# The issue order of a linear attention and Fourier feed-forward kernel, taken from one table of operations, with fewer spare matmuls

## The chip, the cores and the metric

The kernel runs on one core of a Trainium2 chip. The metric is the device time of one launch in microseconds, the median of several runs. Six queues of instructions run side by side on the core and meet through semaphores: TensorE (PE; its weight loads are listed apart as PEld), VectorE (DVE), ScalarE (ACT), GpSimd (POOL), SyncE (SP, which here only issues DMAs) and the 16 DMA engines behind them. Each queue runs its instructions in the order in which the program issued them.

## What is computed

```python
def _attn_ref(q, k, v, g_norm):                  # q, k, v: [8, 8, 576, 64]
    kv = np.einsum('bhsd,bhse->bhde', k, v)
    out = np.einsum('bhsd,bhde->bhse', q, kv)
    rms = np.sqrt(np.mean(out * out, axis=-1, keepdims=True) + 1e-06)
    return out / rms * g_norm

def _moe_ref(x, w_ch1, w_ch2):                   # x: [8, 576, 512]
    mixed = np.real(np.fft.fft(np.fft.fft(x, axis=1), axis=2))
    u = x + mixed
    un = (u - mean(u)) / np.sqrt(var(u) + 1e-06)             # over the channels
    return u + np.maximum(un @ w_ch1, 0.0) @ w_ch2            # 512 x 2048, 2048 x 512
```

The attention output of the eight heads, side by side, is the x of the second part. The two weight matrices arrive as 64-bit floats and are decoded on the chip.

## The kernel before

**Stages.** For each batch, `plan_kv` loads k and v in pieces of 256 KB (L1164) and of 64 KB for the last 64 rows (L1174), multiplies them on PE (ps_k, L1197), copies the result to kvt on ACT and, for batch 0 only, also scales it by g_norm into kvg on DVE (L1216, which needs gb, the loaded g_norm, L1070). `plan_q_load` loads half a batch of q (qt, L1236 and L1247); `plan_q` turns it on PE with an identity matrix (ps_q, L1273) and ACT copies it out (fq). Then come the output products of q with kvt and kvg, per tile of 96 or 97 rows: `plan_first_out` for batch 0 (ps_o, L1374, one group of 16 products into each of two banks with kvt and as many with kvg; three tiles, six groups), `plan_out` for the others (L1304). ACT squares one result, DVE sums the squares (L1391, `red`), takes the inverse root in steps (L1403 to L1411) and multiplies (L1419). `plan_fold` makes even and odd sums of the rows (L1508 on DVE or POOL), each split in a high part (ACT, L1514) and a low part (L1517 on DVE or POOL). `plan_seq` and `plan_chn` multiply them on PE with the tables of the two Fourier transforms (ps_f, L1544 and further lines; the tables are loaded as draw, L1107), and `plan_turn` turns the normalised rows for the feed-forward part, again as a high (unTh, ACT L1693) and a low part (unTl, DVE L1696).

**Weights.** `plan_w` loads one piece of a weight matrix (raw, 512 KB, L936; w1/0, w1/1 and so on for columns of the first matrix, w2/0 and so on for rows of the second) and decodes it: ACT clears a bank, DVE does five steps (L946, L947, L950, L953, L956) and an addition (L1743). For w1 PE then makes the column means (ps_w, L970) and DVE takes them off (L979, the center step). ACT makes the high part (L1763), DVE or POOL the low part (L1768).

**Feed-forward.** ps_h is the product of un and a piece of w1 (L1012), acc that with w2 (L1029), each in three passes over high and low parts. The first of these stands near 79 us in the profile; the attention and the transforms of the later batches run in among them until about 620 us. In the last third, behind that, the feed-forward for the other column pieces runs from stored copies.

**Spare matmuls.** `plan_spare` adds operations that multiply a constant tile (still) by itself twice into a bank that nobody reads (ps_s, 128x512, L1084). The program before has 54 of these matmuls, in 27 pairs.

**What sets the order.** The class `Plan` takes all work of the first two thirds as operations: each has an engine, a cost in ns, a rank, the operations that it needs (`after`) and the buffers that it uses; `MOVES` adds to the ranks of named operations. `run` calls `go`, a list scheduler with a model of the engines, of one pipe of transfers and of buffers that come free; it picks for each engine that is free the operation of lowest rank that can start, and fills in a spare pair where its count of TensorE columns is low. `settle` then moves or drops single operations by the table `SHIFTS`, and `emit` issues the operations in the resulting order. `RINGS` gives the number of buffers of each kind. Each queue waits in hardware for the data and the buffers of the instruction at its head.

Of the kernel before, what the change touches and what calls it, by code (L numbers as in the profile page):

```python
# [76 lines left out]
SHIFTS = [  # L77
    ("plan_spare.go/PE/-/-", 20, 0),
    ("plan_w.<lambda>/DVE/w1/2", 3, -1),
    ("plan_w.<lambda>/DVE/w1/1", 1, -2),  # L80
    ("plan_q.take/ACT/3/11", 0, 2),
    ("plan_spare.go/PE/-/-", 18, 0),
    ("plan_spare.go/PE/-/-", 26, 0),
    ("plan_w.<lambda>/DVE/w2/2", 1, -4),
    ("plan_first_out.mean/DVE/0/1", 0, -2),
    ("plan_chn.<lambda>/DVE/1/1", 1, -6),
    ("plan_spare.go/PE/-/-", 31, 0),
    ("plan_first_out.square/ACT/0/2", 1, 9),
    ("plan_chn.<lambda>/ACT/1/2", 0, 5),
    ("plan_fold.even.go/DVE/1/1", 1, -2),  # L90
    ("plan_fold.fold/DVE/1/0", 0, -6),
    ("plan_spare.go/PE/-/-", 16, 0),
    ("plan_kv.<lambda>/POOL/2/-", 1, 9),
    ("plan_kv.<lambda>/POOL/5/-", 1, -2),
    ("plan_seq.<lambda>/PE/0/1", 0, -1),
    ("plan_turn.high/ACT/0/0", 0, -2),
    ("plan_out.red/DVE/2/1", 1, 10),
    ("plan_seq.<lambda>/PE/0/0", 1, 2),
    ("plan_q_load.load/SP/1/02", 0, 10),
    ("plan_spare.go/PE/-/-", 9, -4),  # L100
    ("plan_fold.mul/DVE/2/0", 0, -4),
    ("plan_q_load.<lambda>/SP/3/-", 0, 1),
    ("plan_spare.go/PE/-/-", 27, 0),
    ("plan_out.<lambda>/ACT/2/1", 0, -1),
    ("plan_kv.<lambda>/DVE/0/-", 0, 9),
    ("plan_fold.zero/ACT/1/1", 0, 4),
    ("plan_out.<lambda>/ACT/2/1", 1, 1),
    ("plan_first.<lambda>/PE/e0/-", 9, 3),
    ("plan_chn.put.<lambda>/SP/0/0", 1, 2),
    ("plan_kv.<lambda>/SP/1/-", 8, 1),  # L110
    ("plan_fold.zero/ACT/2/2", 0, -1),
    ("plan_chn.mix/DVE/0/0", 1, 5),
    ("plan_y.last/DVE/2/-", 0, -1),
    ("plan_seq.<lambda>/PE/0/0", 0, -2),
    ("plan_out.<lambda>/ACT/1/0", 1, 4),
    ("plan_kv.go/PE/1/-", 1, 1),
    ("plan_w.<lambda>/ACT/w2/0", 0, 9),
    ("plan_first.<lambda>/PE/e0/-", 4, 1),
    ("plan_first_out.mean/DVE/0/2", 0, 1),
    ("plan_first_out.mul/DVE/0/1", 0, 1),  # L120
    ("plan_early.<lambda>/ACT/e0/-", 3, -4),
    ("plan_out.scale/POOL/1/2", 0, 8),
    ("plan_chn.<lambda>/DVE/0/0", 0, 1),
    ("plan_kv.<lambda>/SP/5/-", 8, -2),
    ("plan_q.turn/PE/2/12", 0, 1),
    ("plan_fold.fold/DVE/0/2", 0, -2),
    ("plan_kv.<lambda>/POOL/2/-", 0, 9),
    ("plan_spare.go/PE/-/-", 28, 0),
    ("plan_chn.mix/DVE/1/1", 0, -1),
    ("plan_kv.<lambda>/SP/5/-", 3, 4),  # L130
    ("plan_seq.mm/PE/1/3", 0, -2),
    ("plan_turn.high/ACT/0/0", 1, -2),
    ("plan_out.<lambda>/ACT/2/1", 0, 1),
    ("plan_fold.even.go/POOL/2/0", 1, 3),
    ("plan_fold.low/POOL/1/2", 0, -2),
    ("plan_q.take/ACT/2/11", 0, 7),
# [24 lines left out]
    ("plan_spare.go/PE/-/-", 19, 0),
    ("plan_turn.low/DVE/0/1", 2, -1),
    ("plan_first.<lambda>/PE/e0/-", 0, -2),
    ("plan_turn.high/ACT/4/0", 2, 4),
    ("plan_out.red/DVE/2/1", 1, -3),
    ("plan_kv.<lambda>/POOL/3/-", 0, 1),
    ("plan_kv.<lambda>/ACT/6/-", 0, -2),
    ("plan_q.turn/PE/7/02", 0, 1),
    ("plan_chn.add_r/POOL/5/1", 0, -1),
    ("plan_early.<lambda>/ACT/e1/-", 7, 1),  # L170
    ("plan_y.recip/DVE/4/-", 0, -2),
    ("plan_early.<lambda>/ACT/e2/-", 5, -3),
    ("plan_fold.<lambda>/ACT/2/0", 0, -4),
    ("plan_turn.low/DVE/1/2", 0, 3),
    ("plan_out.red/DVE/6/2", 0, 1),
    ("plan_q.take/ACT/7/10", 0, 1),
    ("plan_first.<lambda>/PE/e2/-", 3, -1),
    ("plan_kv.<lambda>/SP/3/-", 9, -3),
    ("plan_out.mm/PE/3/2", 0, 6),
    ("plan_out.scale/POOL/4/2", 0, -3),  # L180
    ("plan_fold.<lambda>/ACT/3/1", 0, 9),
    ("plan_out.mm/PE/4/0", 0, 1),
    ("plan_chn.<lambda>/DVE/2/2", 1, 2),
    ("plan_chn.<lambda>/DVE/4/0", 0, 4),
    ("plan_first.<lambda>/PE/e3/-", 11, -6),
    ("plan_early.<lambda>/PE/e1/-", 7, -1),
    ("plan_early.<lambda>/ACT/e3/-", 3, -3),
    ("plan_out.og/ACT/6/1", 0, -7),
    ("plan_q.take/ACT/4/11", 0, -10),
    ("plan_turn.turn/PE/1/1", 0, 2),  # L190
    ("plan_seq.mm/PE/3/3", 0, 3),
    ("plan_chn.add_l/POOL/5/1", 0, 1),
    ("plan_seq.low/DVE/3/1", 0, -1),
    ("plan_q_load.load/SP/3/-", 0, 4),
    ("plan_kv.<lambda>/SP/4/-", 4, 2),
    ("plan_early.<lambda>/ACT/e1/-", 3, 1),
    ("plan_chn.<lambda>/DVE/0/0", 1, 9),
    ("plan_seq.mm/PE/3/0", 0, 2),
    ("plan_seq.mm/PE/3/2", 0, 3),
    ("plan_fold.<lambda>/ACT/3/1", 0, 4),  # L200
    ("plan_first.<lambda>/ACT/e3/-", 1, -1),
    ("plan_fold.low/DVE/1/1", 0, -1),
    ("plan_seq.<lambda>/ACT/2/1", 0, -2),
    ("plan_q.take/ACT/2/11", 0, -3),
    ("plan_turn.high/ACT/2/0", 3, 2),
    ("plan_turn.high/ACT/3/0", 3, 1),
    ("plan_chn.add_r/POOL/5/1", 0, -1),
    ("plan_out.<lambda>/ACT/6/0", 0, -2),
    ("plan_fold.<lambda>/ACT/1/1", 0, -4),
    ("plan_fold.low/DVE/2/2", 0, -2),  # L210
    ("plan_turn.low/DVE/1/1", 2, -1),
    ("plan_chn.<lambda>/DVE/3/2", 0, -3),
    ("plan_first.<lambda>/ACT/e2/-", 2, -2),
    ("plan_y.last/DVE/2/-", 0, -3),
    ("plan_kv.<lambda>/POOL/4/-", 1, 3),
# [372 lines left out]
class Plan:  # L588

    HOP = 160  # L590
# [5 lines left out]
    SLIP = 100  # L596
# [1928 lines left out]
```

## Time and profile before

| what | value |
|---|---|
| median of 3 runs | 995.82 us (995.66 to 995.9) |
| span of the profiled execution, first to last instruction | 993.5 us |
| TensorE busy | 982.3 us (99%) |
| VectorE busy | 690.1 us (69%) |
| ScalarE, GpSimd busy | 363.4, 397.6 us |
| moved by DMA | 166.06 MB, 167 GB/s on average |

The profile is of one execution. Times are microseconds from the first instruction. In a timeline a row is a run of like instructions: its start, its length, the engine, line, operation, tile names with the shape, the count, and in brackets the idle time ahead of it and what ended that. PEclk is the TensorE clock that the chip granted, 1.00 for 2.4 GHz and 0.50 for 1.2 GHz, as a mean over the stretch.

### The profile page before, as it was taken

The numbers are of one execution on the slowest core, as the hardware profiler recorded it, in microseconds if no ns is written. First come the engines' busy times: TensorE is split into PE (matmuls) and PEld (weight loads), VectorE is DVE, ScalarE is ACT, GpSimd is POOL, SyncE is SP. The second block draws the span as 40 slices with busy tenths as digits, with TensorE's granted clock in tenths as the row PEclk, the third lists the DMA queues.
The fourth block names the chain that finished last, engine by engine and source line by source line (L and its number), as shares of the span: only waits on it lengthen the run. The fifth ranks groups of instructions, "written<-read, shape, count | busy, mean of one in ns | idle before, by whom it ended". The sixth has DMA issues, their size and how long they took to land.

```text
span 993.5 us, 17707 instructions
## 1 busy us (share of the span) xinstructions
PE 982.3 (99%) x6838; PEld 858.5 (86%) x6838; DVE 690.1 (69%) x1365; ACT 363.4 (37%) x731; POOL 397.6 (40%) x391
## 2 busy tenths in 40 slices
PE   8999999999999999999999999999999999999998
PEld 6888989988988888888888898989898888989897
DVE  4889886966667668767843786767676766767543
ACT  2466555655544333333332331323231313122221
POOL 1345443553554101434230372727272727263540
PEclk9899999999999999999999999999999999999999
DMA  9989797764453645565644515151525253424031
GB/s 231 236 222 271 210 275 230 200 161 165 144 195 117 267 168 192 181 252 211 225 170 159 201 44 212 44 212 53 202 81 187 100 171 115 153 107 149 1 127 43
DMA packets 111240, 166.06 MB, mean 167 GB/s; under 512 B 43710, under 2 KB 71666, under 8 KB 104756
## 3 DMA queue, kind: packets, MB, share of 16 engines
q1 hardware_dynamic: 103908, 149.06, 46.9%
q10 hardware_dynamic: 5328, 9.57, 2.6%
q0 software_dynamic: 1920, 6.29, 1.6%
q8 instruction: 54, 0.88, 0.4%
q14 instruction: 30, 0.25, 0.1%
HBM read 108.25 MB, written 56.64 MB: 166 GB/s over the span
## 4 chain that ended last, share of the span: by engine, by line
PE 94%; DMA 3%; SPq 1%; DVE 1%; issue 0%; ACT 0%; DVEq 0%; ACTq 0%
PE acc L1029 40%; PE ps_h L1012 20%; PE ps_h L2251 18%; PE ps_f L1586 4%; PE ps_f L1532 3%; PE ps_o L1304 3%; PE ps_k L1197 2%; PE ps_t L1684 2%; DMA vm<-in_v_dram 1%; PE ps_q L1279 1%; DMA draw<-in_dft_s_dram 1%; DMA qt<-in_q_dram 1%; PE ps_s L1084 1%; PE ps_o L1374 0%; SPq L1174 0%
## 5 line engine op out<-in xcount | busy, mean ns | idle before, releaser
L1029 PE MATMUL acc<-w,hh 128*128 128x512 f32 x1150 | 359.3, 394 | 0.0
L1029 PEld LDWEIGHTS acc<-w,hh 128*128 128x128 f32 x1150 | 205.7, 189 | 34.2
L1029 PE MATMUL acc<-w,hl 128*128 128x512 f32 x575 | 224.0, 390 | 0.0
L1021 ACT ACTIVATE hh<-ps_h 128x512 fp32r<-128x512 f32 x144 | 86.2, 598 | 345.8 <-DVE ps_h L2259 170.9
L1012 PE MATMUL ps_h<-unTh,w 128*128 128x512 f32 x576 | 179.3, 392 | 0.0
L1024 DVE SCALAR_TENSOR_TENSOR hl<-ps_h,hh 128x512 fp32r<-128x512 f32 x144 | 98.0, 684 | 92.1 <-ACT hh L1021 91.8
L1029 PEld LDWEIGHTS acc<-w,hl 128*128 128x128 f32 x575 | 108.0, 188 | 23.6
L1012 PEld LDWEIGHTS ps_h<-unTh,w 128*128 128x128 f32 x576 | 106.6, 188 | 21.3
L1012 PE MATMUL ps_h<-unTl,w 128*128 128x512 f32 x288 | 112.3, 390 | 0.0
L2211 POOL TENSOR_TENSOR up<-up 128x512 f32<-128x512 f32 x36 | 46.6, 1295 | 154.4 <-DMA up<-next_scr 119.2
L2259 DVE TENSOR_TENSOR ps_h<-part,ps_h 128x256 f32<-128x256 f32 x144 | 61.1, 425 | 40.9 <-ACT part L2264 23.3
L2259 DVE TENSOR_TENSOR part<-part,ps_h 128x256 f32<-128x256 f32 x108 | 45.4, 420 | 44.4 <-PE ps_h L2251 41.5
L1012 PEld LDWEIGHTS ps_h<-unTl,w 128*128 128x128 f32 x288 | 54.1, 188 | 11.5
L2224 POOL TENSOR_TENSOR uu<-uu,up 128x512 f32<-128x512 f32 x36 | 46.9, 1312 | 36.9 <-ACT up L2216 36.9
L1353 POOL TENSOR_TENSOR x<-x,gb 96x512 f32<-96x512 f32 (+1 forms) x26 | 33.8, 1311 | 45.0 <-ACT x L1320 45.0
L2264 ACT COPY part<-ps_h 128x256 f32<-128x256 f32 x36 | 13.4, 373 | 81.4 <-PE ps_h L2251 81.4
L1696 DVE TENSOR_TENSOR unTl<-ps_t,unTh 128x384 fp32r<-128x384 f32 (+13 forms) x80 | 34.0, 477 | 9.0 <-ACT unTh L1693 8.9
L2358 DVE SCALAR_TENSOR_TENSOR uu<-acc,bz,uu 128x512 f32<-128x512 f32 x35 | 25.0, 750 | 20.2 <-PE acc L1029 20.2
L1508 POOL TENSOR_TENSOR xe<-ab 96x256 f32<-96x256 f32 (+1 forms) x32 | 25.0, 797 | 34.0 <-DVE ab L1501 32.7
L1340 DVE TENSOR_REDUCE ss<-ps_o 96x8 f32<-96x512 f32 (+1 forms) x42 | 27.9, 682 | 14.1 <-ACT ps_o L1336 13.9
L1586 PE MATMUL ps_f<-cd,pt 128*96 128x258 f32 (+1 forms) x288 | 37.0, 283 | 0.0
L1586 PEld LDWEIGHTS ps_f<-cd,pt 128*96 128x96 f32 (+1 forms) x288 | 35.0, 162 | 1.3 <-DVE ss L1340 0.2
(226 smaller groups left out, 1875.9 us busy)
## 6 DMA issues: line engine op xcount, KB each, us to landing
raw<-in_moe_w_ch_dram SPq DMA_DIRECT2D x32, 512.0 KB, 3.9
unTh<-unT_scr SPq DMA_DIRECT2D x16, 1024.0 KB, 4.9
unTl<-unT_scr SPq DMA_DIRECT2D x16, 1024.0 KB, 7.3
qt<-in_q_dram SPq DMA_DIRECT2D x16, 576.0 KB, 6.7
unT_scr<-unTh SPq DMA_DIRECT2D x9, 1024.0 KB, 3.8
unT_scr<-unTl SPq DMA_DIRECT2D x9, 1024.0 KB, 7.3
part_scr<-part ACTq DMA_DIRECT2D x36, 256.0 KB, 4.0
next_scr<-part SPq DMA_DIRECT2D x36, 256.0 KB, 2.8
```

The costliest lines, as they stand in the source:

```text
L1012: nc.tensor.matmul(ps, w[c][:, kc * P : (kc + 1) * P], unT[a][:, kc, :], start=(kc == 0 and n == 0), stop=(kc == KC - 1 and n == 2),)
L1021: nc.scalar.activation(hh, ps, AF.Relu)
L1024: nc.vector.scalar_tensor_tensor(hl, ps, 0.0, hh.bitcast(F32), ALU.max, ALU.subtract)
L1029: nc.tensor.matmul(acc, hpair[a][:, i * P : (i + 1) * P], w[c], start=(first and n == 0), stop=(last and n == 2),)
L1304: nc.tensor.matmul(pss[s].t[:n, at : at + D], fqs[side].t[half, m, :n], kvt.t[half, m], start=True, stop=True,)
L1353: nc.gpsimd.tensor_tensor(v_, v_, gb[:n].unsqueeze(1).to_broadcast([n, H, D]), ALU.mult)
L1586: nc.tensor.matmul(ps.t[:n, :ND], pt.t[a][:, part, ch, offs[t] : offs[t] + n], cd[:, part, c, ch, :], start=(idx == 0), stop=(idx == 5),)
L1696: nc.vector.tensor_tensor(unTs[j].t[1][:, :, to], view()[:, :, lo:hi], unTs[j].t[0][:, :, to].bitcast(F32), ALU.subtract,)
L2211: lambda p=part: nc.gpsimd.tensor_tensor(p.t[:, 0], p.t[:, 0], p.t[:, 1], ALU.add),
L2224: lambda k=k, ut=ut, p=part: nc.gpsimd.tensor_tensor(ut.t[:, k], ut.t[:, k], p.t[:, 0], ALU.add),
L2251: nc.tensor.matmul(x(to), w.t[:, c, i, kk * P : (kk + 1) * P], rhs(a, kk), start=(kk == 0 and n == 0), stop=(kk == 1 and n == 2),)
L2259: return op("DVE", 415, URGENT, lambda: nc.vector.tensor_tensor(out(), a(), b(), ALU.add), d, bufs)
```

## The change

The tables `SHIFTS` (some 200 rows) and `MOVES` (some 220 rows), the scheduler `go`, its constants and `settle` are gone. In their place stands one table, `ORDER`, that lists the numbers of the operations in the order of issue; `run` looks up each, demands that everything an operation needs stands ahead of it, and hands the list to `emit`, which is as before. The operations themselves, their costs, buffers and instructions are the same, and so is all code of the last third. Line numbers are smaller by 500 in the new file for nearly all code below the class (L1374 is L874 there).

```diff
-SHIFTS = [
-    ("plan_spare.go/PE/-/-", 20, 0),
-    ("plan_w.<lambda>/DVE/w1/2", 3, -1),
...
-]
-MOVES = {
-    "<lambda>/HOST/0/12": 30,
-    "<lambda>/POOL/2": -0.5,
...
-}
+ORDER = """
+5 242 4 221 227 226 381 234 210 209 222 277 393 218 219 230 72 237 232 382 383 384 385 386 387 388 389 27 239
...
+"""
...
 class Plan:
...
-        o.rank = rank + sum(MOVES.get(k, 0) for k in o.key)
...
     def run(self):
-        first = [o for o in self.ops if o.first]
-        if first:
-            self.go(first, False)
-        for o in first:
-            o.aim = o.start
-        return self.go(self.ops, True)
-
-    def go(self, ops, live):
...
-    def settle(self, line):
...
+        seen = set()
+        line = [self.ops[int(n)] for n in ORDER.split()]
+        for o in line:
+            seen.add(o.n)
+            if any(a.n not in seen for a in o.after):
+                raise RuntimeError(f"{o.key} stands ahead of what it needs")
+        self.emit(line)
```

What the list names differs from the old order in two ways. It names six pairs of spare matmuls: 12 stand in the program now, 42 of 54 are left out (one pair after the first turn of q, one ahead of its fourth, three ahead of the k/v products of batch 0, one ahead of the first output product). The counts of all other instructions are the same, and each DMA is on the queue that it was on (418 on SP, 37 on ACT's, 24 on POOL's). And nearly every queue has another order up to the place that the old profile shows at 612 to 619 us; from there on the orders are identical. Three places follow.

SP, the loads of the start. In the old order the rows ahead of these are two raw weights, q and the first pieces of k and v; km and vm, kh and vh are 256 KB pieces of k and v, kr and vr the 64 KB ones, raw a weight. Before:

```order
L1164 DMA km_167<-in_k_dram 128x2x256
L1164 DMA vm_173<-in_v_dram 128x2x256
L1164 DMA km_182<-in_k_dram 128x2x256
L1164 DMA vm_195<-in_v_dram 128x2x256
L1164 DMA kh_208<-in_k_dram 128x2x256
L1164 DMA vh_216<-in_v_dram 128x2x256
L936 DMA raw_229<-in_moe_w_ch1_dram 128x4x256
```

Now:

```order
L436 DMA raw_133<-in_moe_w_ch2_dram 128x1024
L664 DMA km_135<-in_k_dram 128x2x256
L664 DMA vm_137<-in_v_dram 128x2x256
L664 DMA vm_229<-in_v_dram 128x2x256
L674 DMA vr_231<-in_v_dram 64x4x64
L436 DMA raw_233<-in_moe_w_ch1_dram 128x4x256
L674 DMA vr_231<-in_v_dram 64x4x64
L664 DMA vm_236<-in_v_dram 128x2x256
L664 DMA km_238<-in_k_dram 128x2x256
L664 DMA km_240<-in_k_dram 128x2x256
```

The third raw weight (w1/1) stood behind all loads of k and v and now stands ahead of the last four. At the head of the queue, not shown, one piece of k and the first q now stand ahead of the first raw weight, and gb stands behind all of these rows.

DVE, from the last step of w2/0 to the first sums of squares. ps_a, wp and wa are the tiles of a weight's decode, kvg the scaled k/v product, ss the sums. Before:

```order
L1743 TENSOR_TENSOR ps_a_305<-ps_a_305,wp_306 128x512
L1216 TENSOR_TENSOR kvg_363<-ps_k_273,gb_106 128x256
L946 TENSOR_SCALAR ps_a_385<-ps_a_385 128x512
L947 TENSOR_SCALAR ps_a_385<-ps_a_385 128x512
L1768 TENSOR_TENSOR w20_389<-ps_a_305,w20_389 128x512
L1391 TENSOR_REDUCE ss_113<-ps_o_368 96x2x4
L1391 TENSOR_REDUCE ss_113<-ps_o_367 96x2x4
L950 SCALAR_TENSOR_TENSOR ps_a_385<-raw_229,ps_a_385 128x512
```

Now:

```order
L1243 TENSOR_TENSOR ps_a_294<-ps_a_294,wp_295 128x512
L446 TENSOR_SCALAR ps_a_305<-ps_a_305 128x512
L447 TENSOR_SCALAR ps_a_305<-ps_a_305 128x512
L450 SCALAR_TENSOR_TENSOR ps_a_305<-raw_233,ps_a_305 128x512
L453 TENSOR_SCALAR wp_306<-ps_a_305 128x512
L456 SCALAR_TENSOR_TENSOR wp_306<-raw_233,wp_306 128x512
L1268 TENSOR_TENSOR w20_310<-ps_a_294,w20_310 128x512
L1243 TENSOR_TENSOR wa_307<-ps_a_305,wp_306 128x512
L716 TENSOR_TENSOR kvg_322<-ps_k_251,gb_106 128x256
L891 TENSOR_REDUCE ss_113<-ps_o_327 96x2x4
```

The whole decode of w1/1 moved ahead of kvg and of the sums; before, two of its steps stood ahead of the sums and the others among them and behind. Its center step (L979) moved ahead of the last fold of batch 0's first half, and with it POOL's low part of w1/1 (L1768) no longer stands ahead of the even and odd sums that the first sequence transform waits for.

PE, the last k/v products of batch 0 and the first output product. ps_s is a pair of spares. Before:

```order
L1197 MATMUL ps_k_273<-vm_195,km_182 64x64 x8
L1197 MATMUL ps_k_273<-vr_160,kr_121 64x64 x2
L1084 MATMUL ps_s_327<-still_107 128x512 x2
L1084 MATMUL ps_s_333<-still_107 128x512 x2
L1197 MATMUL ps_k_273<-vh_216,kh_208 64x64 x8
L1197 MATMUL ps_k_273<-vr_160,kr_121 64x64 x2
L1084 MATMUL ps_s_349<-still_107 128x512 x2
L1084 MATMUL ps_s_358<-still_107 128x512 x2
L1374 MATMUL ps_o_367<-kvt_274,fq_186 96x64
```

Now:

```order
L584 MATMUL ps_s_226<-still_107 128x512 x2
L697 MATMUL ps_k_251<-vh_129,kh_117 64x64 x8
L697 MATMUL ps_k_251<-vr_231,kr_126 64x64 x2
L697 MATMUL ps_k_251<-vm_137,km_135 64x64 x8
L697 MATMUL ps_k_251<-vr_231,kr_126 64x64 x2
L697 MATMUL ps_k_251<-vm_236,km_238 64x64 x8
L697 MATMUL ps_k_251<-vr_231,kr_126 64x64 x2
L697 MATMUL ps_k_251<-vm_229,km_240 64x64 x8
L697 MATMUL ps_k_251<-vr_231,kr_126 64x64 x2
L584 MATMUL ps_s_324<-still_107 128x512 x2
L874 MATMUL ps_o_327<-kvt_252,fq_164 96x64
```

The four k/v products now follow each other; seven pairs of spares among and behind them have become one.

## Rows read from the trace of the kernel before

**Rows 1.** The page: busy us of each engine, share of the span, instructions

```profile
PE 982.3 (99%) x6838; PEld 858.5 (86%) x6838; DVE 690.1 (69%) x1365; ACT 363.4 (37%) x731; POOL 397.6 (40%) x391
```

**Rows 2.** Windows: stretch, length, busy by engine (count), clock, DMA share, GB/s

```profile
0.00:25.00 25.00, 20.84 (x232) 16.40 (x234) 10.01 (x18) 6.80 (x13) 3.37 (x13) 1.00 0.93 231
25.00:55.00 30.00, 28.23 (x422) 25.05 (x419) 24.96 (x47) 14.14 (x31) 11.57 (x13) 0.89 1.03 239
55.00:78.00 23.00, 22.70 (x354) 20.58 (x354) 21.52 (x49) 16.21 (x39) 8.79 (x12) 1.00 0.81 214
35.00:40.00 5.00, 5.00 (x42) 4.04 (x40) 3.55 (x10) 2.56 (x7) 2.51 (x2) 0.50 1.19 180
90.00:300.00 210.00, 210.00 (x1950) 186.41 (x1946) 154.35 (x321) 117.94 (x275) 102.04 (x125) 1.00 0.66 203
300.00:560.00 260.00, 260.00 (x1204) 216.76 (x1203) 179.84 (x287) 93.55 (x170) 67.42 (x66) 1.00 0.54 194
560.00:620.00 60.00, 58.86 (x365) 52.70 (x364) 42.54 (x88) 15.68 (x29) 26.85 (x21) 1.00 0.41 144
```

**Rows 3.** Timeline of TensorE at the borders of the start's stages

```profile
9.34 1.55 PE L1273 MATMUL ps_q<-ident,qt 96*64 96x96 f32 x32 [0.59 <-DMA qt<-in_q_dram]
...
22.54 0.69 PE L1197 MATMUL ps_k<-vh,kh 128*64 128x64 f32 x16
...
24.40 1.57 PE L1374 MATMUL ps_o<-kvt,fq 64*96 64x64 f32 x32
25.81 1.53 PE L1374 MATMUL ps_o<-kvg,fq 64*96 64x64 f32 x32
...
34.69 1.45 PE L1374 MATMUL ps_o<-kvg,fq 64*96 64x64 f32 x14
...
37.51 0.79 PE L1084 MATMUL ps_s<-still 128*128 128x512 f32 x1
...
54.62 0.54 PE L1544 MATMUL ps_f<-cs,xh 97*128 97x290 f32 x2
...
78.81 0.73 PE L1012 MATMUL ps_h<-unTh,w 128*128 128x512 f32 x2
```

**Rows 4.** Windows of the spares alone (ps_s): PE, PEld busy, clock, DMA

```profile
0.00:10.00 10.00, 7.05 (x18) 5.22 (x18) 1.00 0.75 215
10.00:26.00 16.00, 4.79 (x16) 2.69 (x16) 1.00 1.06 238
26.00:56.00 30.00, 4.56 (x12) 2.48 (x12) 0.89 1.01 237
56.00:90.00 34.00, 1.80 (x6) 1.05 (x6) 1.00 0.89 236
```

**Rows 5.** Timelines of VectorE, ScalarE and GpSimd: decode, w1/1, last low part

```profile
28.43 0.68 DVE L950 SCALAR_TENSOR_TENSOR ps_a<-raw,ps_a 128x512 uint32<-128x512 uint32 x1
42.84 1.19 DVE L956 SCALAR_TENSOR_TENSOR wp<-raw,wp 128x512 f32<-128x512 uint32 x1
47.32 0.67 DVE L979 TENSOR_TENSOR wa<-wa,ps_w 128x512 f32<-128x512 f32 x1
48.03 0.63 ACT L1763 ACTIVATE w<-wa 128x512 fp32r<-128x512 f32 x1 [3.88 <-DVE wa L979]
48.74 1.27 POOL L1768 TENSOR_TENSOR w<-wa,w 128x512 fp32r<-128x512 f32 x1 [3.24 <-ACT w L1763]
23.80 0.42 DVE L1216 TENSOR_TENSOR kvg<-ps_k,gb 128x256 f32<-128x256 f32 x1 [1.94 <-ACT kvt L1208]
76.69 1.42 DVE L1696 TENSOR_TENSOR unTl<-ps_t,unTh 128x384 fp32r<-128x384 f32 x4
```

**Rows 6.** DMA issues of the page: count, KB each, us from issue to landing

```profile
raw<-in_moe_w_ch_dram SPq DMA_DIRECT2D x32, 512.0 KB, 3.9
qt<-in_q_dram SPq DMA_DIRECT2D x16, 576.0 KB, 6.7
km<-in_k_dram SPq DMA_DIRECT2D x31, 256.0 KB, 4.2
```

More of the change, by code (lines that the diff above doesn't have):

```diff
@@ L588 @@
 class Plan:
-    HOP = 160
-    DRAIN = 120
-    MARGIN = {"PE": 500}
-    AHEAD = 6000
-    LAND = 2200
-    ISSUE = 450
-    SLIP = 100
-    BEGIN = {"PE": 1700, "SP": 300, "ACT": 300, "DVE": 800, "POOL": 800}
-    WARM = 6600
-    COLS = {730: 1536, 880: 1200, 1760: 2560, 440: 576, 1500: 1024, 400: 650, 1200: 1950, 760: 1548, 681: 1536, 460: 1024, 920: 1024}
-    TICK, FULL = 3414, 3400
+    ISSUE = 450
     def __init__(self, rings):
@@ L604, in __init__ @@
         self.ops = []
-        self.now = 0
         self.where = ("-", "-")
@@ L609, in op @@
         o = Op()
-        o.port = port or eng == "POOL"
-        o.wait = wait
         o.eng, o.cost, o.emit, o.lag = eng, cost, emit, lag
@@ L620, in op @@
         o.dma = o.first = False
-        o.aim = None
         self.ops.append(o)
@@ L796, in settle @@
-    def settle(self, line):
-        named = {}
-        for o in self.ops:
-            named.setdefault(o.key[1], []).append(o)
-        for key, k, n in SHIFTS:
-            o = named[key][k]
-            if o not in line:
-                continue
-            if not n:
-                line.remove(o)
-                continue
-            step = 1 if n > 0 else -1
-            at = i = to = line.index(o)
-            while n:
-                i += step
-                if not 0 <= i < len(line) or o in line[i].after or line[i] in o.after:
-                    break
-                if line[i].eng == o.eng:
-                    n -= step
-                    to = i
-            line.insert(to, line.pop(at))
-        return line
+        seen = set()
```

630 lines of the change are left out of this document (removed), and 179 rows, old and new, of the table ORDER.

## The prediction

> **What bounds the kernel now.** I read the page first, then the windows by stage, then TensorE's timeline at the stage borders, then the other engines there. The page shows TensorE busy for 982.3 of 993.5 us [rows 1]; the next engine, VectorE, for 690.1. So the span can shrink in three ways only: less work on TensorE, less of it at half clock, fewer gaps. The windows say where such time lies [rows 2]. From 90 to 560 us TensorE is busy for 210.00 of 210.00 and 260.00 of 260.00 us at clock 1.00: nothing waits there and nothing but removed matmuls can help. From 560 to 620 it is busy for 58.86 of 60, one gap of 1.14. From about 619 us on the two orders are the same. What can be gained lies before 90 us: there TensorE has gaps (20.84 of 25, 28.23 of 30, 22.70 of 23), a stretch at half clock (0.50 from 35 to 40 us), and almost all of the spare matmuls [rows 4].
>
> The start has three phases, seen in TensorE's timeline [rows 3]. Until 24.40 us it waits for data: the first turn of q (L1273) starts at 9.34, the last k/v product of batch 0 at 22.54, the first output product (L1374) at 24.40. From there to the first FFN matmul (L1012) at 78.81 are 54.4 us. After it TensorE never lacks work. So I predict one moment, the first FFN matmul, and then add what happens behind it.
>
> **What TensorE itself needs from 24.40 to 78.81.** Take from 54.4: gaps 2.1 (1.77 of the window 25 to 55 and 0.30 of 55 to 78 [rows 2]); spares 4.56, and 0.7 of the 1.80 of the last window, since four of that window's six run behind 78.81 [rows 4]; and what the low clock took: the window 25 to 55 was granted 0.89 on average, 6.6 of its 30 us at half speed, so 3.3. That leaves 43.7. The spares from 37.51 on are counted twice, as spares and as half-clock time, which puts about 1 back: some 45 us. The same operations stand between these two points in both orders, so 45 is the bound after the change too.
>
> **The change, part by part.**
> *Spares.* 42 of 54 matmuls go. Those ahead of 24.40 filled time in which TensorE waited for loads (7.05 + 4.79 us [rows 4]); taking them out gains nothing by itself. Those between 24.40 and 78.81 (5.3 us) shorten TensorE's need, which decides only if TensorE is what sets 78.81. Those behind 78.81 are pure work on the bound: four around 79.61 and two near 255 us, together 1.8 us less the 0.7 before, plus the pair near 255 (half of the four's price): **−1.4 us**.
>
> *The queue of loads (SP).* Ahead of the last k/v load of batch 0 stood two raw weights (512 KB each [rows 6]), q (two of 576 KB), gb (32 KB) and k/v: 4514 KB. Now three raw weights stand there and gb doesn't: 4997 KB, +483 KB. At the 231 GB/s of this window [rows 2] that is **+2.1 us** on the last k/v product and so on the first output product: 22.5 becomes 24.6. ACT's copy to kvt comes behind, in the new order with one copy of q more behind it, so I put the first output product at 26.8, between 26.5 (only the bytes) and 27.2. Earlier in the queue the first q lands sooner, 834 KB with it instead of 1602 KB; that lets the turns of q start before 9.34, in time that nothing needs.
>
> *VectorE's order.* Ahead of kvg (L1216, 23.80 us) and of the first sums of squares now stands the whole decode of w1/1 that before stood at 28.43 and 42.84 us [rows 5], and the low part of w2/0: six steps of the 0.68 us of the one at 28.43 and one of 1.19, together 5.3 us. It goes into time in which VectorE idles: in the first 25 us it is busy for 10.01 us [rows 2], so it costs nothing as long as the third raw weight lands in time; it stands 4 loads from the end of the k/v loads, which speaks for that. If that load is late, kvg is late behind it, at most by the 5.3 us. What it gives back comes later: the steps at 28.43 and 42.84 are no longer between the sums of the first outputs. The center step (L979) stands ahead of the last fold; before, it ended at 47.99, ACT waited 3.88 for it and POOL then 3.24 [rows 5], and the even/odd sums ahead of the sequence transform stood behind this on POOL until 50.0, so that the sequence transform began at 54.62 [rows 3]. In the new order these sums don't stand behind it, and I put the transform at about 48.
>
> *Who is late next.* With these gone VectorE sets the pace: its work up to the last low part (76.69 us, L1696) is 10.01 + 24.96 + 21.52 less 0.7 that lies behind, 55.8 us [rows 2, 5]; its idle time there is 21.5 us, 15.0 in the first window, 5.0 and 1.5 in the others. In the new order 1.9 us more work stand ahead of that point (a center step of w1/2, 0.7, three low parts, 1.4, and a small step, 0.5, less one sum of 0.7), 57.7. Idle time before the first sum of squares stays: it comes about 2 us behind the first output product, at 28.8, and VectorE has 15 us of work by then, so it idles 13.7. Behind it idle lies between 0 and the 5.4 that the windows show now with the 1.1 of before 25 us. So the last low part ends between 57.7 + 13.7 = 71.4 and 76.8. I take 4.0 of idle, nearer to what the windows show than to none, since turns and low parts alternate between three engines: 75.4, and the first FFN matmul 0.7 later (76.69 + 1.42 to 78.81 [rows 3, 5]), at 76.1: **−2.7 us**. TensorE's own need allows 26.8 + 45 = 71.8, so it would wait some 4 us in this stretch.
>
> *90 to 620 us.* Nearly every queue has another order here. Nothing can be gained but the two spares already counted [rows 2]. A loss is possible at each of the many hand-overs, since the order is now the list's and a load that waits for its buffer holds the loads behind it on SP. The nearest row is the 1.14 us gap in 560 to 620 [rows 2]. It may vanish (−1.1), or two more of its size may come (+2.3). I take **+0.5**.
>
> **Sum.** −2.7 − 1.4 + 0.5 = −3.6, the 2.1 of the loads being inside the −2.7. On the span of 993.5 that is 989.9. The median of the runs, 995.82, is 2.3 above the span of the profiled execution; with it 992.2.
>
> **Rivals.**
> *R1, slower: the clock.* Seven pairs of spares stood among the k/v products and right behind them; now three pairs stand ahead of all k/v products and one between these and the first output product. The trace shows what the clock does to these products: one group takes 25.81 − 24.40 = 1.41 us at 2.4 GHz, and 2.82 (34.69 to 37.51) at 1.2 GHz [rows 3], and from 35 to 40 the clock stayed at 0.50 although TensorE was busy for 5.00 of 5.00 us [rows 2], spares from 37.51 on among it. If TensorE is at 1.2 GHz when kvt is ready, nothing wide follows to raise it: six groups cost 6 × 1.41 = 8.5 more, two turns and the mean of w some 2 more. The bound is then 26.8 + 45 + 10.5 = 82.3 or, with the wait for the last load, 83, against 78.81: +4.2, less 1.4: 993.5 + 2.8 + 2.3 = 998.6. It is decided at one point, the granted clock at the first output product. For it: gaps among the k/v products are now empty. Against it: the one pair just ahead, and that the group at 25.81 kept the full clock with no spare since 24.40.
>
> The Trainium skill, TensorE: Matmul & The Clock Gate, in "What's actually happening", says that "the default state is throttled, and activity releases the throttle". This speaks against taking the spares out ahead of the output products; the trace agrees in that the stretch of small products from 34.69 on was granted 0.50. By that rule alone the sum would be R1's 998.6; by the rows at 24.40 and 25.81, full clock on such products, it stays at 992.2.
>
> *R2, no change.* The start's 2.1 us later loads are not won back: VectorE's idle of 5.4 stays and the low clock from 34.69 on stays, or the loads behind (weights, DFT tables) come later than the compute wants them, at 1.03 of DMA share in 25 to 55 us [rows 2]. The first FFN matmul then stays at 78.8, and only the spares behind it are won: −1.4, 994.4, say 994.5.
>
> *R3, faster.* VectorE has no idle time behind the first sum and TensorE's need decides: 71.8, and the sum is −7.0 − 1.4 + 0.5 = −7.9: 993.5 − 7.9 + 2.3 = 987.9, and 988.5 with the 0.6 us that TensorE's own hand-overs cost it. For it: 1.5 us of idle in the last window.
>
> *R4, slower: SP in order.* A load that waits for a buffer holds back k/v or weight loads somewhere in 90 to 620 us, and TensorE, which has no slack there, waits four times 1.14 us on top of the forecast: 997 and more. Against it: DMA share 0.66 and 0.54 there [rows 2].
>
> **How the numbers follow.** Forecast 0.40, with its own range 990 to 994 (2 us either way by the idle of VectorE from 2 to 5.4 and the gaps of 90 to 620). R3 0.12, R2 0.22, R1 0.22, R4 0.04. The range reaches from 988.8, which leaves half of R3 out, to 998.8, which has most of R1 in it. A measurement of this kernel tells about 0.2%, 2 us, from no change: the bounds are 993.8 and 997.8. The forecast and R3 are faster, R2 and a few of the forecast's highest are the same, R1 and R4 slower: 0.52, 0.22, 0.26.
>
> **What the trace of the changed kernel will show.** The last k/v product at about 24.6 and the first output product at 26.8 (loads); the granted clock at the first output group 1.00 and 1.41 us a group (against R1: 2.82); sequence transform at about 48; first FFN matmul at 76 with TensorE waiting some 4 us for VectorE between 27 and 76 (R3: at 72 with no wait; R2: at 78 to 79); windows 90 to 300 and 300 to 560 still full. The prediction is wrong in its step on the clock if groups last 2.82, in its step on VectorE if the first FFN matmul comes at 72 or 79, and in its step on loads if the first output product comes before 25 or behind 28.

## The result, and the profile after

The changed kernel takes 1008.37 us (median of 4, 1006.79 to 1011.11) against 995.86: 1.013 times as long, with an interval of 1.0111 to 1.0149. It is slower; the forecast was 992.2, and the range ended at 998.8. The profiled execution has a span of 1006.1 us against 993.5, so 12.6 us are to be found.

The windows of the changed kernel (columns as in rows 2) show where:

```profile
25.00:55.00 30.00, 28.22 (x358) 26.83 (x358) 21.36 (x45) 12.38 (x27) 8.13 (x10) 0.60 0.61 157
...
90.00:300.00 210.00, 209.19 (x1971) 187.37 (x1969) 153.81 (x316) 114.45 (x272) 98.61 (x125) 1.00 0.66 200
300.00:560.00 260.00, 259.93 (x1210) 216.43 (x1209) 180.62 (x292) 91.49 (x169) 69.32 (x69) 1.00 0.56 196
560.00:620.00 60.00, 56.09 (x322) 49.34 (x321) 35.88 (x78) 16.05 (x30) 26.02 (x21) 0.97 0.41 133
620.00:700.00 80.00, 77.73 (x469) 69.39 (x469) 58.36 (x130) 20.99 (x38) 38.70 (x31) 0.98 0.41 135
```

From 25 to 55 us TensorE is as busy as before (28.22 against 28.23 [rows 2]), but at a granted clock of 0.60 instead of 0.89. From 560 us on it has gaps of 3.9 and 2.3 us, where the old kernel had 1.1 from 560 to 620 [rows 2] and none from 620 to 700, and a clock of 0.97 and 0.98.

For the comparison of two orders I count TensorE's work: the spares left out, each operation at the median duration of its kind in the old kernel's trace. The table gives how many us later than the old kernel each kernel reaches the same amount of work (negative: earlier), worked out from the traces, so from one execution of each; e1 and the others are the experiments below.

```
TensorE work done (us)    after    e1    e2   e11   e17   e13    e7
  9  (first outputs)       +3.6  +3.5  +0.3  -0.2  -0.4  +0.5  +3.7
 15                        +8.6  +6.1  +0.6  +2.4  +2.2  +3.1  +8.7
 55  (first FFN matmuls)   +3.6  -2.6  -1.4  -6.8  -7.5  -5.1  +3.5
120  (about 150 us)        +3.3  -0.4  -0.7  -5.4  -6.9  -4.2  +5.0
530  (about 565 us)        +3.6  -0.7  -1.1  -4.8  -6.7  -3.4  +4.6
560  (about 600 us)        +7.6  +3.5  -1.7  -0.8  -2.9  -4.1  +5.0
620  (about 670 us)       +12.6  +6.0  -1.7  +3.1  +1.0  -4.1  +7.4
```

So there are two losses: 3.6 us up to the first FFN matmuls, and 9.0 between 565 and 650 us. Between them nothing is lost, and behind them nothing. TensorE's timeline at the first one and at the second, and then the windows of 4 us at the second:

```profile
23.39 0.29 PE L697 MATMUL ps_k<-vr,kr 128*64 128x64 f32 x4
23.61 0.73 PE L584 MATMUL ps_s<-still 128*128 128x512 f32 x2
26.78 4.10 PE L874 MATMUL ps_o<-kvt,fq 64*96 64x64 f32 x48 [2.43 <-ACT kvt L708]
30.67 1.49 PE L874 MATMUL ps_o<-kvt,pt 64*96 64x64 f32 x16
...
582.47 1.45 PE L1751 MATMUL ps_h<-w,w1p(10, 11)_5454 128*128 128x256 f32 x6 [2.64 <-DVE ps_h L1759]
...
636.29 0.50 PE L1751 MATMUL ps_h<-unTh,w1p(10, 11)_5454 128*128 128x256 f32 x2 [2.13 <-DVE part L1759]
```

```profile
582.00:586.00 4.00, 3.53 (x12) 3.05 (x13) 3.47 (x8) 0.99 (x2) 3.75 (x3) 0.59 0.10 10
...
636.00:640.00 4.00, 3.57 (x16) 3.05 (x17) 3.90 (x10) 1.13 (x2) 3.27 (x3) 0.67 0.23 56
```

The 64 products from 26.78 on take until 31.95, 2.6 us for a group of 32 that took 1.41 before [rows 3]: TensorE waited 2.43 us for kvt and came out of it at 1.2 GHz. The two late waits are again followed by a low clock, which about doubles what they cost.

### The profile page after: what moved, and what is told of

The parts are those of the page before. It is cut to its first block, busy times and chain, and to the rows that moved or that the text cites. A ratio compares the mean times of both kernels' runs of the same rounds, so it can differ in the third digit from the quotient of the medians.

```text
span 1006.1 us, 17543 instructions
## 1 busy us (share of the span) xinstructions
PE 982.3 (98%) x6796; PEld 862.5 (86%) x6796; DVE 686.3 (68%) x1365; ACT 357.9 (36%) x731; POOL 392.5 (39%) x391
## 4 chain that ended last, share of the span: by engine, by line
PE 86%; DVE 4%; DMA 3%; issue 3%; POOL 2%; SPq 1%; ACT 1%; DVEq 0%; POOLq 0%; ACTq 0%
PE acc L529 37%; PE ps_h L512 18%; PE ps_h L1751 17%; PE ps_f L1032 3%; PE ps_f L1086 3%; PE ps_o L804 2%; DMA qt<-in_q_dram 2%; PE ps_o L874 2%; PE ps_k L697 1%; PE ps_q L779 1%; PE ps_t L1184 1%; DMA out_dram<-uu 1%; PE ps_q L773 1%; SPq L664 1%; PE ps_w L470 0%
## 5 line engine op out<-in xcount | busy, mean ns | idle before, releaser
L529 PEld LDWEIGHTS acc<-w,hh 128*128 128x128 f32 x1150 | 208.0, 190 | 36.1 <-DVE x L990 0.9
L1759 DVE TENSOR_TENSOR part<-part,ps_h 128x256 f32<-128x256 f32 x108 | 45.4, 420 | 48.3 <-PE ps_h L1751 45.4
L446 DVE TENSOR_SCALAR ps_a<-ps_a 128x512 f32<-128x512 f32 x32 | 22.2, 694 | 29.5 <-ACT ps_a L439 29.4
L1196 DVE TENSOR_TENSOR unTl<-ps_t,unTh 128x384 fp32r<-128x384 f32 (+16 forms) x80 | 34.5, 471 | 10.8 <-ACT unTh L1193 10.7
L1193 ACT ACTIVATE unTh<-ps_t 128x384 fp32r<-128x384 f32 (+16 forms) x80 | 33.2, 488 | 9.8 <-PE ps_t L1184 8.4
```

The costliest lines, as they stand in the source:

```text
L529: nc.tensor.matmul(acc, hpair[a][:, i * P : (i + 1) * P], w[c], start=(first and n == 0), stop=(last and n == 2),)
L1193: nc.scalar.activation(unTs[j].t[0][:, :, to], view()[:, :, lo:hi], AF.Copy)
L1196: nc.vector.tensor_tensor(unTs[j].t[1][:, :, to], view()[:, :, lo:hi], unTs[j].t[0][:, :, to].bitcast(F32), ALU.subtract,)
L1759: return op("DVE", 415, URGENT, lambda: nc.vector.tensor_tensor(out(), a(), b(), ALU.add), d, bufs)
```

## The experiments on the late loss

All kernels are the changed file with another `ORDER`; the diffs show the numbers of operations in it. Behind each time stand in brackets its ratio to the old kernel, timed beside it, and the 95% interval of that ratio. Line numbers in them are some 20 lower than in the changed kernel.

**e3 and e4: one part of the order alone.** e3 has the changed order up to TensorE's place at 420 us and the old one behind, e4 the reverse.

> The changed order up to TensorE's place at 420 us, from there on the operations that are left in the old order. Theory A (two separate losses: 3.6 us in the start, 9.0 between 565 and 650 us, the latter by the new order of the weight work and row loads on GpSimd, SyncE and VectorE behind 420 us): the second goes, 1008.4 - 9.0 = 999.4 us. Theory C (the late loss follows from the shift that the start hands on, not from the order there): 1008.

> The old order up to TensorE's place at 420 us with all its spares, from there on what is left in the changed order. Theory A (the order behind 420 us makes the late loss by itself): 995.9 + 9.0 = 1004.9 us, with TensorE waiting for VectorE at L1751 as in the changed kernel. Theory C (the late loss comes from the start's shift): 996.

e3 took 999.05 us (1.0037, 1.0023 to 1.0051), e4 1003.52 (1.008, 1.0061 to 1.0099). TensorE's waits in e4 (engine, line, releaser: us in total, times, longest), and the window of e3:

```profile
PE ps_h L1731 <- DVE ps_h L1739: 3.9, 3, 2.6
PE ps_b L1614 <- DVE dg L1606: 2.3, 1, 2.3
...
PE ps_h L1731 <- DVE part L1739: 1.9, 1, 1.9
```

```profile
560.00:620.00 60.00, 59.54 (x352) 52.60 (x351) 40.90 (x81) 17.53 (x31) 26.16 (x21) 1.00 0.45 166
```

The late loss goes with the order behind 420 us: with it behind an undisturbed start the same waits are there, 3.9 us at the same line, and without it they are gone. Theory C, that the start's shift makes it, is out.

**e7: two moves.** Which instructions wait is seen on VectorE and SyncE of the changed kernel:

```profile
579.86 1.28 DVE L1643 TENSOR_TENSOR unTh<-unTh,ps_b 128x512 fp32r<-128x512 f32 x2 [1.08 <-PE ps_b L1634]
...
581.99 0.42 DVE L1759 TENSOR_TENSOR ps_h<-part,ps_h 128x256 f32<-128x256 f32 x1
```

```profile
629.07 0.33 SPq L1705 DMA_DIRECT2D up<-part_scr  x1
629.51 0.37 SPq L1569 DMA_DIRECT2D uu<-u_scr  x1
```

The addition at 581.99, for which TensorE stands still since 579.8, reads products that end by 579.6 but is listed behind multiplications that themselves wait for TensorE. The load of uu, whose statistics come ahead of the additions for which TensorE waits until 636.29, stands on SP behind a load of up that is held until 629.07; in the old order uu stood ahead of up (issued at 611.57 and 612.08).

```diff
-... 2776 2778 2719 2724 2722 2779 2721 2777 ...
+... 2776 2778 2719 2779 2777 2724 2722 2721 ...
-... 2886 2979 2896 ...
+... 2886 2896 2979 ...
```

> The changed kernel with two moves behind 570 us: on VectorE the last two additions of a product's even and odd part (L1759) ahead of the first normalising multiplication (L1643) that waits for TensorE, instead of behind it; on SyncE the load of rows of u (uu) ahead of the load of up that is held back by its buffer. Theory D (these two in-order waits are the late loss: 2.64 and 2.13 us of waiting, and about as much again by the clock behind each): 8 us shorter than the changed kernel, some 1000. Theory E (the late order is late as a whole, and the next wait takes their place): 1004 to 1008.

1002.49 us (1.0053, 1.0033 to 1.0072): 5.9 below the changed kernel's median. In the table the late loss falls from 9.0 to 2.8. TensorE's waits there are 1.9 us instead of 3.9, and the clock of 560 to 620 is 1.00:

```profile
PE ps_h L1730 <- DVE ps_h L1738: 1.9, 3, 0.9
...
PE ps_b L1613 <- DVE dg L1605: 1.3, 1, 1.3
```

Theory D has most of it; its time of some 1000 us was not quite reached. 2.8 us are left, and these smaller waits are what the trace shows for them; no run took them out one by one.

## The experiments on the start

**e1: more spares.** Five more pairs in the 2.43 us ahead of the first output product.

```diff
-... 64 243 245 ...
+... 64 6 7 8 9 10 243 245 ...
```

> The changed order with five more pairs of spares on TensorE, right ahead of the first output product (in the 2.43 us in which TensorE waited for kvt there); nothing else differs. Theory A (the clock: TensorE idles ahead of the first output products, starts them at 1.2 GHz and stays there until about 52 us): the groups take 1.41 us instead of 2.8, the granted clock of 25 to 55 us is 0.95 or more instead of 0.60, and of the some 11 us of half-clock time there most comes back: 999 us, between 997 and 1004, the rest going into waits for VectorE. Theory B (the order itself is slow in the start, VectorE and the loads set its pace, and the clock only fills time in which TensorE would wait anyway): 1007 to 1009 as for the changed kernel. The loss of 9 us between 565 and 650 us stays under both.

1003.92 us (1.0096, 1.0075 to 1.0117). The window, and the first output products:

```profile
25.00:55.00 30.00, 26.92 (x454) 24.04 (x453) 28.51 (x55) 17.57 (x38) 14.18 (x18) 1.00 0.71 192
...
27.94 2.25 PE L854 MATMUL ps_o<-kvt,fq 64*96 64x64 f32 x48 [0.47 <-ACT kvt L688]
```

The clock is back (1.00), the first FFN matmul comes at 77.15 instead of 83.28, and the start is 2.6 us ahead of the old kernel instead of 3.6 behind. Behind that 2 us go to loads (1.5 us of waiting for km). So the low clock is the start's loss; that spares are the cure doesn't follow yet. The 1003.92 us is the upper edge of what theory A said, and the cure isn't certain either: the trace is of the shortest of the four executions (1001.56, mean clock 0.998), and in the two longest (1005.81 and 1004.87) the mean clock was 0.989 and 0.990.

**e2: the old order without 42 spares.**

> The old order with 42 of its 54 spares left out; the 12 kept stand at the places that they have in the changed order (one pair after the first turn of q, one ahead of a later turn, three ahead of the first k/v product, one ahead of the first output product). Theory A (leaving the spares out costs the clock at the first output products): the six groups of them take 2.8 us each, the first FFN matmul comes 4 to 9 us later than 78.8, and with 1.4 us won behind it the time is 998 to 1004. Theory B (the order was at fault, not the spares): 994 to 996, since the removed matmuls only filled waiting time or gave 1.4 us back.

993.49 us (0.9979, 0.9965 to 0.9993), a little faster than the old kernel. Its first output group starts at 24.72, right behind the last spare, and takes 1.40 us; the clock of 25 to 55 is 0.83 (0.89 in the old kernel [rows 2]):

```profile
24.72 1.57 PE L853 MATMUL ps_o<-kvt,fq 64*96 64x64 f32 x32
```

```profile
25.00:55.00 30.00, 27.58 (x423) 25.71 (x420) 27.24 (x51) 15.42 (x32) 12.31 (x14) 0.83 0.97 240
```

Theory A was wrong here: leaving the spares out costs this order nothing on balance. Its copy to kvt ends at 24.53, before the one pair behind the last k/v product does, so TensorE doesn't wait.

**e5, e6, e9: make the wait go by order.** In the changed kernel ScalarE's copy to kvt stands behind the high part of w2/0:

```profile
20.44 0.63 ACT L439 ACTIVATE ps_a<-raw 128x512 f32<-128x512 f32 x1 [2.02 <-PE ps_s L584]
...
25.48 0.60 ACT L1263 ACTIVATE w<-ps_a 128x512 fp32r<-128x512 f32 x1 [3.05 <-DVE ps_a L1243]
...
26.33 0.39 ACT L708 COPY kvt<-ps_k 128x256 f32<-128x256 f32 x1
```

```diff
-... 404 231 401 240 224 236 405 406 407 408 409 402 410 225 64 243 ...
+... 404 231 224 401 240 236 405 406 407 408 409 402 410 225 64 243 ...   (e5: kvt)
+... 404 231 224 401 240 236 225 405 406 407 408 409 402 410 64 243 ...   (e6: kvt, kvg)
+... 404 231 236 224 401 240 225 405 406 407 408 409 402 410 64 243 ...   (e9: fq, kvt, kvg)
```

> The changed kernel with one move: on ScalarE the copy to kvt stands ahead of the high part of w2/0 (in the changed kernel it stands behind it and behind one copy of q, at 26.33 us, though the last k/v product ends at 23.68). No spare is added. If the cause of the low clock is this one late copy (theory A1), the first output product comes at 24.4 instead of 26.78, runs at 1.41 us a group, and then TensorE waits some 3 us for kvg, which VectorE makes at 30.14; what the clock does behind that wait is open: 1000 to 1005 us. If the missing spares by themselves keep TensorE at 1.2 GHz there (theory A2), the groups still take 2.8 us: 1006 to 1009.

> The same, and on VectorE the scaled product kvg stands ahead of the decode of w1/1 instead of behind it. Theory A1: no wait is left among the first output products, they run at 2.4 GHz, and the start is 4 to 6 us shorter than in the changed kernel, as with the five pairs of spares: 1001 to 1004 us, the late loss of 7 to 9 us being still there. Theory A2: 1006 to 1009.

> The changed kernel, on ScalarE the copy of q (fq) that the first output product needs and the copy to kvt ahead of the high part of w2/0, on VectorE kvg ahead of the decode of w1/1. No spare added. In the run with kvt and kvg alone TensorE still waited 1.86 us for that fq between the first 16 output products (at 2.4 GHz) and the next 32 (at 1.2). Theory A1 (a wait of some 2 us ahead of these small products is what costs the clock): no wait is left, the groups take 1.41 us throughout, granted clock of 25 to 55 us 0.95 or more, 1000 to 1003 us, the late loss still in it. Theory A2 (12 spares are too few whatever stands behind them): clock 0.6 to 0.8 there and 1004 to 1008.

1004.23 us (1.0076, 1.0052 to 1.0099), 1005.87 (1.0091, 1.0055 to 1.0127) and 1004.84 (1.0092, 1.0074 to 1.011): each 2.5 to 4 below the changed kernel. e5 lies inside the range of A1, e6 just below that of A2, e9 inside that of A2, with the clock of 0.72 that A2 said. They don't decide between the two, since none of them is without a wait. The timelines of e6 and, behind the dots, of e9 show why:

```profile
24.65 1.02 PE L853 MATMUL ps_o<-kvt,fq 64*96 64x64 f32 x16
27.52 2.83 PE L853 MATMUL ps_o<-kvt,fq 64*96 64x64 f32 x32 [1.86 <-ACT fq L762]
```

```profile
30.95 1.70 PE L853 MATMUL ps_o<-kvg,fq 64*96 64x64 f32 x30 [2.62 <-DVE w L1247]
33.97 1.57 PE L853 MATMUL ps_o<-kvt,fq 64*97 64x64 f32 x16 [1.32 <-ACT fq L762]
```

Each move uncovered the next wait: the first 16 products of e6 run at 2.4 GHz, then comes a wait of 1.86 us for a copy of q, and the next 32 run at 1.2; in e5 it is the same with 1.78 us. In e9 TensorE waits 2.62 us for a bank that VectorE's decode of w2/0 still reads. The moves treated what stands behind this decode, not why it is late.

e8 and e10 are e6 and e9 with the two late moves:

> All four moves together. Theories A1 and D: 1008.4 - 5 - 8 = 995, within 992 to 997, about the old kernel's time; what is won beyond that by the 42 spares and the earlier start is held back by the loads of k and q near 85 us, as with the five pairs of spares (TensorE waited 1.5 us for km there). Otherwise over 1000.

> The same with the two late moves (even and odd additions ahead of the normalising multiplications on VectorE, the load of uu ahead of the held-back load of up on SyncE), which took 6 us off the changed kernel by themselves. A1: 994 to 997, the old kernel's time. A2: 998 to 1002.

They took 1001.81 us (1.0051, 1.0032 to 1.007) and 1000.74 (1.0047, 1.0032 to 1.0061), both longer than A1 said (992 to 997 and 994 to 997) and e10 inside A2's range, with a clock of 0.60 and 0.66 from 25 to 55 us in the profiled executions. e12, the spares of e1 with the two late moves, took 998.96 (1.0022, 1.0003 to 1.0042), as both together should:

> The changed kernel with five more pairs of spares ahead of the first output product and with the two late moves. Both losses are treated, each by what worked alone: 1003.9 - 6 = 998, between 995 and 1000. If the two losses share a cause, less than either: over 1001.

**e11 and e16: fewer spares.** A bank here is one of eight buffers that the program hands out in the order of the table; an operation that is given one waits until its last user is done. ScalarE's clear at 20.44 waits 2.02 us for a spare: the decode of w2/0 is given the bank that one of the three pairs ahead of the k/v products writes into. In the old kernel this clear ran without a wait, and the copy to kvt stood right behind it:

```profile
16.86 0.62 ACT L939 ACTIVATE ps_a<-raw 128x512 f32<-128x512 f32 x1
23.39 0.37 ACT L1208 COPY kvt<-ps_k 128x256 f32<-128x256 f32 x1 [5.92 <-PE ps_k L1197]
```

e11 leaves these three out, e16 the other three.

```diff
-... 239 228 235 49 17 70 216 ...
+... 239 228 235 216 ...            (e11; e16 takes out 72, 27 and 64 instead)
```

> The changed kernel without the three pairs of spares that stand ahead of the first k/v product, so with 6 spares instead of 12; nothing else differs. In the changed kernel ScalarE's clear for w2/0 waits 2.02 us for a bank that one of these pairs holds, and the decode, the high part and the copy to kvt come later by it. Theory A1: the copy to kvt comes about 2 us earlier, at 24.3 to 24.7, TensorE's wait ahead of the first output product is under 1 us, and the time is not longer than the changed kernel's, 1002 to 1008, although spares are taken away. Theory A2 (spares are what keeps the clock): clock low from the k/v products on, 1008 to 1012.

> The control: the changed kernel without the other three pairs (the first, the second, and the one right ahead of the first output product), the three ahead of the k/v products kept; again 6 spares. Theory F (it is these three pairs, not the number of spares): the clear for w2/0 still waits for their bank, kvt is late, the clock low: 1004 to 1009, as the changed kernel. If any three pairs less do (theory H): about 1000.

e11: 1000.52 us (1.005, 1.0031 to 1.007); e16: 1006.09 (1.0105, 1.0088 to 1.0122). The clear and the copy to kvt on ScalarE and the first output product on TensorE, e11 first:

```profile
17.85 0.66 ACT L418 ACTIVATE ps_a<-raw 128x512 f32<-128x512 f32 x1
23.77 0.39 ACT L687 COPY kvt<-ps_k 128x256 f32<-128x256 f32 x1
24.22 2.25 PE L853 MATMUL ps_o<-kvt,fq 64*96 64x64 f32 x48 [0.99 <-ACT kvt L687]
```

```profile
18.99 0.63 ACT L418 ACTIVATE ps_a<-raw 128x512 f32<-128x512 f32 x1 [1.54 <-PE ps_s L563]
24.88 0.39 ACT L687 COPY kvt<-ps_k 128x256 f32<-128x256 f32 x1
25.33 4.11 PE L853 MATMUL ps_o<-kvt,fq 64*96 64x64 f32 x48 [3.34 <-ACT kvt L687]
```

Six spares instead of twelve, and 8 us less, where it is the right six; e11 is even below what A1 said, e16 is where theory F put it. Without the three pairs the clear doesn't wait, TensorE waits 0.99 us, the groups run at 2.4 GHz, and the first FFN matmul comes at 72.90. That is the profiled execution. Of the ten, three had a mean clock of 0.988, as low as in the changed kernel (0.984 to 0.988), and took 1001.95 to 1004.58 us: some of the gain is there even so.

**e17: the bank alone.** All 12 spares, every engine's order as in the changed kernel; only the place in the table of the three pairs and of the k/v products is behind the clear. That changes which bank the clear is given, and also the banks of the spares and the products that it now stands ahead of.

```diff
-... 235 49 17 70 216 ... 223 220 214 217 238 394 395 ...
+... 235 216 ... 238 394 49 17 70 223 220 214 217 395 ...
```

> The changed kernel with the same 12 spares and the same order of instructions on every engine; only the place in the table at which the three pairs of spares and the first k/v products are listed comes behind ScalarE's clear for w2/0, so that the clear is given its bank first and no longer the one that a spare pair holds. Theory F (the bank): the clear starts at 18 to 19 us instead of 20.44 and kvt comes up to 2 us earlier; if the spares and the k/v products then wait for a bank themselves, part of it is lost: 999 to 1004. Theory I (the three pairs cost by their place on TensorE, not by the bank): 1006 to 1010 as the changed kernel.

996.81 us beside an old kernel of 994.5 (1.0032, 1.0007 to 1.0058), where the changed kernel stands at 1.013:

```profile
17.62 0.66 ACT L418 ACTIVATE ps_a<-raw 128x512 f32<-128x512 f32 x1
23.55 0.39 ACT L687 COPY kvt<-ps_k 128x256 f32<-128x256 f32 x1
23.99 2.25 PE L853 MATMUL ps_o<-kvt,fq 64*96 64x64 f32 x48 [0.69 <-ACT kvt L687]
```

This settles it: the same instructions in the same order on every engine, the banks handed out to the clear first, and the start is 7.5 us ahead of the old kernel where it was 3.6 behind. It is more than theory F said (999 to 1004). The late loss is in it still. Nine of the ten executions took 995.27 to 1000.18 us, one 1005.14 at a mean clock of 0.990.

**e13, e14, e15: both losses out.** e13 is e11 with the old order behind 420 us, e14 that without any spare, e15 e11 with the two late moves.

> The changed order up to 420 us without the three pairs of spares ahead of the first k/v product (6 spares left), the old order behind 420 us. Theory F (the three pairs hold the bank that the decode of w2/0 waits for; the delay ends in TensorE's wait for kvt and the low clock): the start keeps the 5 us that it was ahead of the old kernel without them, the late loss is gone: 995.6 - 5 = 991, between 989 and 994, faster than both kernels. If the start's gain is lost again behind (theory G, the old order behind 420 us can't use it), 994 to 997.

> The same without any spare. Theory F: spares matter by the banks they hold and by what else fills a wait, so the time is about that of the run before, 989 to 995. Theory A2 (a few spares are needed to hold the clock through the k/v and first output products): the clock of 25 to 55 us falls to 0.6 to 0.8 and the time is 996 to 1001.

> The changed kernel without the three pairs and with the two late moves on VectorE and SyncE. Theory F with theory D: 1000.5 - 6 = 994.5, between 992 and 998.

e13 takes 991.34 us (0.9949, 0.9932 to 0.9965): faster than both kernels, at a clock of 1.00 in all four executions. e14: 996.8 (1.0011, 0.9999 to 1.0022); there TensorE waits 1.72 us for kvt and the clock of 25 to 55 is 0.66, so the last three pairs are worth 5.5 us there. The time and the clock are what A2 said, and theory F's 989 to 995 missed. But without the pairs the banks are handed out differently again, and TensorE has a second wait, of 1.17 us for the bank of a decode, that e13 lacks: whether the 5.5 us are the pairs' own work or their banks is not shown. Of e13, and behind the dots of e14:

```profile
24.94 2.25 PE L853 MATMUL ps_o<-kvt,fq 64*96 64x64 f32 x48 [1.05 <-ACT kvt L687]
...
26.32 1.74 PE L853 MATMUL ps_o<-kvt,fq 64*96 64x64 f32 x34 [1.72 <-ACT kvt L687]
29.23 1.06 PE L853 MATMUL ps_o<-kvt,fq 64*96 64x64 f32 x10 [1.17 <-DVE w L1247]
```

```profile
25.00:55.00 30.00, 27.41 (x502) 24.91 (x504) 28.63 (x54) 17.97 (x39) 13.85 (x17) 1.00 0.79 215
...
25.00:55.00 30.00, 27.51 (x376) 26.05 (x378) 21.54 (x45) 13.08 (x29) 8.64 (x13) 0.66 0.66 165
```

e15: 996.79 (1.0015, 0.9992 to 1.0038). Its times go from 992.55 to 1002.0 with mean clocks from 1.000 to 0.985: how much of its clock TensorE keeps differs from one execution to the next. Where the executions without a trace lost it is not shown.

## Why the prediction was wrong

Two steps failed: the choice between the forecast and R1 on the clock of the first output products, and the +0.5 us for 90 to 620 us, which came out as +9.0.

**What bounds the kernel**: right. Nothing was won or lost from 90 to 560 us, and TensorE's gaps and clock are the whole difference.

**The spares' term, −1.4**: about right. e2 measures all 42 spares, in the old order, at −2.1 us (0.9979, so −3.5 to −0.7).

**Loads, and the first output product at 26.8**: the moment was right (26.78) for a wrong reason, by luck. The last k/v product started at 22.88, not 24.6, although a third raw weight stood ahead: the +2.1 us of the loads came out as +0.3 (22.54 before [rows 3]), and in the first 25 us the transfers ran at 245 GB/s, not the 231 that were taken. TensorE then waited 2.43 us for kvt. The sentence that failed is that ACT's copy comes with one copy of q more behind the k/v product. It also stands behind the high part of w2/0, and with it behind the whole decode of w2/0; I read VectorE's side of that decode and not ScalarE's, and no row of the old trace has a clear that waits for a spare's bank (there it ran at 16.86).

**The clock**: the forecast chose the wrong side. R1's numbers came: groups of 2.6 to 2.8 us, as it priced (2.82), and the first FFN matmul at 83.28, where R1 had 82.3 to 83. It had 0.22 because the group at 25.81 kept the full clock without spares. But this group had no wait ahead of it; the question was whether there would be one. R1's reason, spares taken out, is not what made the wait: e17 has the same 12 spares and held the clock in its trace. The Trainium skill, TensorE: Matmul & The Clock Gate, "What's actually happening", names the throttled state as the default; the trace agrees in so far as the changed kernel came out of its 2.43 us of idle time at 1.2 GHz.

How long a wait costs TensorE its clock, these runs don't show. Right behind waits of 0.47 to 1.05 us (e1, e17, e11, e13) and of 1.71 and 1.72 (e15, e14) the small products ran at 2.4 GHz in the profiled executions, behind 1.78, 1.86, 2.43 and 3.34 us (e5, e6, the changed kernel, e16) at 1.2. But in e9 they ran at 2.4 behind 2.62 us, and the clock fell while they ran, ahead of the next wait: it was 1.00 from 30 to 32 us and 0.62 from 32 to 33. And it was 0.53 from 33 to 44 us in e2 and 0.50 from 35 to 40 in the old kernel [rows 2], where the longest wait among the output products was 0.92 and 1.17 us.

**VectorE's pace and the first FFN matmul at 76.1**: in e1, with the clock held, it came at 77.15 and the start was 2.6 us ahead by the same work (forecast: 2.7). In e17, with kvt 2.8 us earlier too, it came at 72.27, and the start was 7.5 us ahead; R3 had 71.8. From its first sum of squares (27.69) to there VectorE idles 1.2 us in all, where the forecast took 4.0. TensorE's need of 45 us was right as well: from 23.99 to 72.27 it is busy for 45.4 and waits 2.9. That the sum still meets R3's moment is part luck, since the first output product came 2.8 us before R3's 26.8. The new order of the start was worth what the best case said; a bank took it away. One reading was wrong: the old kernel's sequence transform began at 46.75, and the row at 54.62 is its first product with 97 rows. That product, put at about 48, came at 57.24 in the changed kernel and at 46.56 in e17.

**90 to 620 us, +0.5**: the step that was most mis-sized. It measured +9.0, of which 4.2 came at 636 us, behind the place from which on the orders are the same: a load that is exchanged ahead of that place held its data back until then. I priced new hand-overs by the one gap of 1.14 us that the old order had, and took two more of its size as the upper end. The new order has gaps of 2.64 and 2.13 us behind in-order waits of VectorE and SP, and each was followed by a low clock, which the term didn't hold at all. R4 named SP's in-order wait, but at 0.04 and with 4 × 1.14 us, without the clock.

**The range** ended at 998.8, R1 alone. The two losses are independent (e3 and e4 have one each: +3.6 and +8.0 us by the medians beside them), and no case had both.

## What to carry to other kernels

A rotating buffer that a filler instruction writes can be a wait for whoever gets it next: before adding or moving fillers, look at which bank they are given and who follows. When an order is replaced as a whole, price the places where two engines wait for each other in turn, and not only the mean of the old gaps; a wait of TensorE there can cost, beside its length, a stretch at half clock behind it (from 27 to 50 us in the changed kernel). And a good part can hide in a slow whole: with the old order behind 420 us and three pairs of spares less, this order gave a kernel of 991.34 us against 995.3.

## What was not expected of the hardware

The cost of the two late waits on TensorE was about twice their length: 2.64 us at 582.47 went with 4.4 us of delay (from 3.2 to 7.6 by the same work), 2.13 us at 636.29 with 4.2 (from 8.4 to 12.6). And one clear that got its bank 2.02 us late went with 11 us of delay by the first FFN matmul (3.6 behind in the changed kernel against 7.5 ahead in e17, one execution of each).
